# Attention, a SoLU layer and a top-1 expert layer on one core: w_out centred over its rows, the norm's factor applied after the second product, h as one tile over two PSUM banks

## The chip, the cores and the metric

One core of a Trainium2 chip runs the whole program. The metric is device time in microseconds (us), the median of three runs. Engines: TensorE (PE; its weight loads are listed as PEld), VectorE (DVE), ScalarE (ACT), GpSimd (POOL), and SyncE (SP), which only issues transfers. Each engine works through its own list of instructions in a fixed order.

## The reference, cut to what matters

```python
attn = softmax(mask(q @ k.T / 8)) @ v            # 4 batches, 8 heads, 768 positions, 64 wide
x = attn.reshape(3072, 512)
h = x @ w_in                                      # 512 -> 1024
e = np.exp(h - h.max(-1)); sm = e / (e.sum(-1) + 1e-9)
solu = h * sm
ln = (solu - solu.mean(-1)) / np.sqrt(solu.var(-1) + 1e-6) * g_ln
x = ln @ w_out                                    # 1024 -> 512
idx = argmax(x @ w_gate); gate = softmax(x @ w_gate)[idx]
out = gate * (relu(x @ w1[idx]) @ w2[idx])        # 8 experts
```

## The kernel before, in words

**Attention** works in 32 units (two heads, half a batch's positions). A unit is scores, row maximum (L226 on VectorE), exponential (L228 on ScalarE), transposes, product with v. Its result x is split into a high and a low part (bxh, bxl, L302 and L303).

**The SoLU layer** ("MoE 1") works in 24 tiles of 128 tokens. `m_in` multiplies x with w_in in two halves of 512 columns, three matmuls per slice for the high and low parts (L426 to L428); each half of the result is a PSUM bank of its own, `h`. `m_act` takes the row maximum of each half (L432), the exponential (L443), h times it (L445), the mean, the squares (L451, which write over h), then y = 1/sqrt(variance) with a Newton step, and in L460 the normalised e = e*y + mean*y. `m_tr` transposes e (L475) and splits it into lh and ll (L478, L479). `m_out` multiplies with w_out (L496 to L498), whose 264 columns hold 256 of w_out and 8 router logits in the first half; L504 to L512 are the router's small vector steps; `m_route` ranks the token within its expert (L521, L522). `m_in` runs two tiles ahead of `m_out`.

**Weights** arrive as 64-bit floats. `decode` (L316 to L333) fetches 512 KB, and rebuilds 32-bit values on VectorE, ScalarE and GpSimd. `load_w_in` and `load_w_out` split them into high and low parts (wih and wil, woh and wol). `load_w_out` also scales by g_ln (L370, L371), transposes w_out (L349) and multiplies it with w_gate (L357), so that the logits come out of the same matmul.

**The experts** ("MoE 2") follow: `f_in` (L779 to L781) and `f_out` (L828 to L830).

**Order.** The generators `attention()`, `moe1()` and `weights()` are stepped in turn. For the first 110 attention steps (C0) only attention and weights are stepped: w_in's eight steps first, one in six attention steps (WSTEP), then w_out's from step 62 (C1). After that attention and MoE 1 share by a ratio (RATIO). A scheduler that reckons with a timeline of its own then sets each engine's order. PSUM has 8 banks; `ps` hands out 3 to the tag "psa" (attention) and 5 to "psm" (MoE 1 and decoding), and rotates over both in the experts.

Of the kernel before, what the change touches and what calls it, by code (L numbers as in the profile page):

```python
# [29 lines left out]
NPT, XBUFS, QKB, PKB, VB = 2, 8, 2, 2, 2  # L30
WB, DB, EB, NXR, XGB = 3, 4, 2, 2, 6
PA = 3
NATP = 3
KLV = 2
LA = 2
# [5 lines left out]
C0, C1, WSTEP, WSTEP2, RATIO = 110, 62, 6, 2, 0.7  # L41
# [11 lines left out]
def body(ctx, tc, a):  # L53
# [6 lines left out]
    ps_p = ctx.enter_context(tc.tile_pool(name="ps", bufs=8, space=PSUM))  # L60
# [3 lines left out]
    def open_moe1(where, sfx):  # L64
# [4 lines left out]
        wil = w1p.tile([128, 4, DF], F32R, name="wil" + sfx)  # L69
# [239 lines left out]
    wg_sb = const.tile([128, 4, NE], F32, name="wg_sb")  # L309

# [5 lines left out]
    def decode(src, sb=None):  # L316
# [15 lines left out]
        V.scalar_tensor_tensor(out=y, in0=x, scalar=E_MIN, in1=t.bitcast(F32), op0=ALU.is_ge, op1=ALU.mult)  # L332
        return y  # L333

    def load_w_in():
        for k in range(4):
# [7 lines left out]
    def load_w_out():  # L344
        def logits(k, x):

            t = ps("wt")
            for d in range(4):
                T.transpose(t[:, 128 * d:128 * d + 128], x[:, 128 * d:128 * d + 128], ident)  # L349
            xt = dec_tile("xt").bitcast(F32).rearrange("p (a b) -> p a b", a=4)  # L350
            A.activation(out=xt, in_=t.rearrange("p (a b) -> p a b", a=4), func=AF.Copy)
            return k, xt

        def logits2(k, xt):
            t = ps("wt2")
            for d in range(4):
                T.matmul(t[:, 0:NE], xt[:, d, :], wg_sb[:, d, :], start=(d == 0), stop=(d == 3))  # L357
            wp = t[:, 0:NE]
            gk = g_sb[:, k:k + 1]
            V.tensor_scalar(out=woh[:, k, 0, 256:264], in0=wp, scalar1=gk, scalar2=None, op0=ALU.mult)  # L360
            V.scalar_tensor_tensor(out=wol[:, k, 0, 256:264], in0=wp, scalar=gk, in1=raw(woh)[:, k, 0, 256:264],
                                   op0=ALU.mult, op1=ALU.subtract)

        last = last2 = None
        for k in range(8):
            x = dec_tile("dec").bitcast(F32)
            decode(a["w_out"].bitcast(I32)[128 * k:128 * k + 128, :], x)
            h_ = woh[:, k, :, 0:256]
            p2 = x.rearrange("p (a b) -> p a b", a=2)
            A.activation(out=h_, in_=p2, func=AF.Copy, scale=g_sb[:, k:k + 1])  # L370
            V.scalar_tensor_tensor(out=wol[:, k, :, 0:256], in0=p2, scalar=g_sb[:, k:k + 1], in1=raw(h_),  # L371
                                   op0=ALU.mult, op1=ALU.subtract)
            if last2:
                logits2(*last2)
                last2 = None
            if last:
                last2 = logits(*last)
            last = (k, x)
# [40 lines left out]

    def m_in(t, c):  # L420
        xh, xl = xs_t[t]
        h = ps("h")
        h_t[t, c] = h
# [6 lines left out]
        if c == 0:  # L430
            sc_t[t] = mp.tile([128, 12], F32, tag="sc", name="sc", bufs=LA)
        V.tensor_reduce(out=sc_t[t][:, c:c + 1], in_=h, axis=AX.X, op=ALU.max, negate=True)  # L432
# [3 lines left out]
    def m_act(t):  # L436
        sc = sc_t.pop(t)
        nm, sm, mu, v_, y, w_, es = [sc[:, j:j + 1] for j in (0, 2, 4, 6, 8, 9, 10)]
# [841 lines left out]
```

## Time and profile before

| | us |
|---|---|
| median of 3 runs | 839.29 (838.95 to 845.25) |
| the profiled execution | 835.08 |
| its span | 833.4 |
| TensorE busy in it | 783.8 (94%) |
| VectorE, ScalarE, GpSimd busy | 469.0, 470.7, 380.0 |

The span is the time between the first and the last recorded instruction; the profiled execution's own time is 1.7 us longer. A matmul's end is modelled, so a busy TensorE isn't one at its peak. Granted clock 1.00 is TensorE's 2.4 GHz, 0.50 is 1.2 GHz. In a row of waits the engine before the arrow sat idle until the instruction behind it ended.

### The profile page before, as it was taken

How to read it: one execution, taken by the hardware profiler on the slowest of the kernel's cores; microseconds unless marked ns; L12 is line 12 of the kernel's file. 1: busy time of each engine (PE TensorE's matmuls, PEld its weight loads, DVE VectorE, ACT ScalarE, POOL GpSimd, SP SyncE). 2: the span in 40 equal slices, each digit the busy share in tenths (PEclk: the TensorE clock that was granted, in tenths of full speed). 3: DMA queues.
4: the chain of work that ended last, by engine and by line, in shares of the span. 5: the costliest groups of instructions: out<-in, count | busy, mean ns of one | idle time of the engine just before them, and what ended most of it. 6: DMA issues, size and time to landing. Idle time of an engine off the chain costs nothing.

```text
span 833.4 us, 15246 instructions
## 1 busy us (share of the span) xinstructions
PE 783.8 (94%) x4906; PEld 681.7 (82%) x4906; DVE 469.0 (56%) x1730; ACT 470.7 (56%) x1224; POOL 380.0 (46%) x419
## 2 busy tenths in 40 slices
PE   3479999899999999999999989999999999999996
PEld 2258888788898887888988879989988898989885
DVE  6779674776757747666776475425414332435421
ACT  4686685676766847757766364235314342435532
POOL 4777356454544554545443021157225253526433
PEclk9986999999999999999999999999999999999999
DMA  8687456677555557564431270286325353536320
GB/s 271 194 208 184 104 157 96 174 136 141 143 138 143 126 117 149 134 148 122 126 75 40 22 246 27 54 279 224 115 89 171 101 176 117 174 116 201 129 103 18
DMA packets 77385, 114.36 MB, mean 137 GB/s; under 512 B 14125, under 2 KB 53485, under 8 KB 77296
## 3 DMA queue, kind: packets, MB, share of 16 engines
q1 hardware_dynamic: 69456, 91.02, 42.6%
q0 software_dynamic: 5248, 13.88, 4.7%
q10 hardware_dynamic: 2592, 8.39, 3.0%
q8 instruction: 41, 0.67, 0.4%
q14 instruction: 48, 0.39, 0.3%
HBM read 72.22 MB, written 13.94 MB: 103 GB/s over the span
## 4 chain that ended last, share of the span: by engine, by line
PE 77%; DMA 10%; DVE 5%; issue 4%; ACT 2%; POOL 1%; POOLq 0%; SPq 0%; ACTq 0%; DVEq 0%
PE x L496 5%; PE ht L780 5%; PE ht L779 5%; PE ht L781 5%; PE x L498 5%; PE x L497 5%; PE y L830 5%; PE h L426 5%; PE y L829 5%; PE y L828 5%; PE av L297 5%; PE h L427 5%; PE h L428 4%; PE s L221 3%; DMA w<-w_in 2%
## 5 line engine op out<-in xcount | busy, mean ns | idle before, releaser
L496 PE MATMUL x<-woh,lh 128*128 128x264 f32 (+1 forms) x384 | 112.0, 292 | 0.5 <-DVE ll L479 0.4
L228 ACT ACTIVATE P<-P,mx 128x144 f32<-128x144 f32 x192 | 78.7, 412 | 55.5 <-DVE mx L226 52.9
L498 PE MATMUL x<-woh,ll 128*128 128x264 f32 (+1 forms) x384 | 110.0, 287 | 0.0
L497 PE MATMUL x<-wol,lh 128*128 128x264 f32 (+1 forms) x384 | 109.4, 285 | 0.0
L700 POOL TENSOR_TENSOR wl<-wst,wh 128x1024 fp32r<-128x1024 f32 x28 | 68.5, 2445 | 63.2 <-ACT wh L694 63.0
L694 ACT ACTIVATE wh<-wst 128x1024 fp32r<-128x1024 f32 x64 | 67.5, 1058 | 46.5 <-PE ht L780 33.9
L828 PE MATMUL y<-wh,hh 128*128 128x512 f32 x224 | 89.8, 401 | 0.0
L830 PE MATMUL y<-wh,hl 128*128 128x512 f32 x224 | 88.1, 395 | 0.1
L829 PE MATMUL y<-wl,hh 128*128 128x512 f32 x224 | 87.6, 392 | 0.0
L700 DVE TENSOR_TENSOR wl<-wst,wh 128x1024 fp32r<-128x1024 f32 x36 | 54.7, 1526 | 51.1 <-ACT wh L694 51.0
L780 PE MATMUL ht<-xel,wh 128*128 128x288 f32 (+5 forms) x256 | 81.2, 318 | 0.0
L781 PE MATMUL ht<-xeh,wl 128*128 128x288 f32 (+5 forms) x256 | 81.0, 318 | 0.0
L779 PE MATMUL ht<-xeh,wh 128*128 128x288 f32 (+5 forms) x256 | 79.7, 318 | 0.0
L426 PE MATMUL h<-wih,bxh 128*128 128x512 f32 x192 | 78.1, 407 | 0.8 <-DVE ll L479 0.8
L186 POOL TENSOR_TENSOR lA<-qd,qA 128x384 fp32r<-128x384 f32 x29 | 29.7, 1024 | 105.1 <-ACT qA L184 104.5
L225 DVE COPY_PREDICATED s<-pick,s 128x128 f32<-128x128 int32 x160 | 45.5, 292 | 54.2 <-PE s L222 51.7
L427 PE MATMUL h<-wil,bxh 128*128 128x512 f32 x192 | 76.0, 396 | 0.0
L496 PEld LDWEIGHTS x<-woh,lh 128*128 128x128 f32 x384 | 72.9, 190 | 1.8 <-DVE ll L479 0.5
L428 PE MATMUL h<-wih,bxl 128*128 128x512 f32 x192 | 73.9, 398 | 0.0
L497 PEld LDWEIGHTS x<-wol,lh 128*128 128x128 f32 x384 | 73.0, 190 | 0.8
L498 PEld LDWEIGHTS x<-woh,ll 128*128 128x128 f32 x384 | 72.8, 190 | 0.4 <-issue 0.2
L835 ACT ACTIVATE y<-y,gate 128x512 f32<-128x512 f32 x28 | 19.3, 688 | 92.9 <-PE y L830 69.4
(243 smaller groups left out, 2094.4 us busy)
## 6 DMA issues: line engine op xcount, KB each, us to landing
wst<-w SPq DMA_DIRECT2D x64, 512.0 KB
x_d<-xrow SPq DMA_DIRECT2D x24, 264.0 KB
qd<-qT SPq DMA_DIRECT2D x32, 192.0 KB
qB<-qA SPq DMA_DIRECT2D x58, 96.0 KB
lB<-lA SPq DMA_DIRECT2D x58, 96.0 KB
kd<-kx SPq DMA_DIRECT2D x16, 280.0 KB
w<-w_in ACTq DMA_DIRECT2D x8, 512.0 KB
w<-w_out ACTq DMA_DIRECT2D x8, 512.0 KB
```

The costliest lines, as they stand in the source:

```text
L426: T.matmul(h, xh[k], wih[:, k, cs], start=(k == 0), stop=False)
L427: T.matmul(h, xh[k], wil[:, k, cs], start=False, stop=False)
L496: T.matmul(p[:, 0:n], lh[:, k, :], woh[:, k, c, 0:n], start=(k == 0), stop=False)
L497: T.matmul(p[:, 0:n], lh[:, k, :], wol[:, k, c, 0:n], start=False, stop=False)
L498: mm = T.matmul(p[:, 0:n], ll[:, k, :], woh[:, k, c, 0:n], start=False, stop=(k == 7))
L700: return (G if c % 2 and r else V).tensor_tensor(out=l_, in0=st_w.pop((r, which, c)), in1=raw(h_), op=ALU.subtract)
L779: T.matmul(o, wh[:, k, fs], xh(k), start=(k == 0), stop=False)
L780: T.matmul(o, wh[:, k, fs], xl(k), start=False, stop=False)
L781: T.matmul(o, wl[:, k, fs], xh(k), start=False, stop=(k == 3))
L828: T.matmul(o, hh[:, k, sl], wh, start=(k == 0), stop=False)
L829: T.matmul(o, hh[:, k, sl], wl, start=False, stop=False)
L830: T.matmul(o, hl[:, k, sl], wh, start=False, stop=(k == 7))
```

## The change

- w_out is decoded first into an 8-slice tile (wox) that shares its memory with wil; the mean over its 1024 rows of g*w_out is made on TensorE (`mean`: g/1024 broadcast as weights), and each slice is centred (`xc`) before it is split. The logit columns are centred in the same way. w_in is decoded after that. Steps come one in four attention steps, 24 in all.
- With a centred w_out the mean of solu need not be subtracted: `m_act` leaves out L459 and L460, and the factor y is applied where ScalarE copies the second product out (scale=y) and in the router's shift.
- h is one tile of 1024 columns over two PSUM banks, in a buffer of its own (tag "psh", one buffer); the maximum, exponential, product and square are one instruction each instead of two.
- The router's small tensors L and M lie in spare columns of the product's PSUM bank.
- PSUM: "psa" 3 banks, "psm" 3, "psh" 2, where the experts use psh's two halves in turn.

```diff
-PA = 3
-C0, C1, WSTEP, WSTEP2, RATIO = 110, 62, 6, 2, 0.7
+C0, WSTEP, WSTEP2, RATIO = 110, 4, 2, 0.7
...
+        return ps_p.tile([128, 512], F32, tag=tag, name=name, bufs=3)
+    def ps2(name):
+        return ps_p.tile([128, 1024], F32, tag="psh", name=name, bufs=1)
...
     def load_w_out():
+        mn = ps2("mn")
+        x8 = w1p.tile([128, 8, 2, 256], F32, tag="wil", name="wox")
...
+        def mean(k, out, x):
+            T.matmul(out, g_m[:, k:k + 1].to_broadcast([128, 128]), x, start=(k == 0), stop=(k == 7),
+                     skip_group_check=True)
...
+        for k in range(8):
             h_ = woh[:, k, :, 0:256]
-            A.activation(out=h_, in_=p2, func=AF.Copy, scale=g_sb[:, k:k + 1])
-            V.scalar_tensor_tensor(out=wol[:, k, :, 0:256], in0=p2, scalar=g_sb[:, k:k + 1], in1=raw(h_),
-                                   op0=ALU.mult, op1=ALU.subtract)
+            xc = ps("xc")
+            V.scalar_tensor_tensor(out=xc.rearrange("p (a b) -> p a b", a=2), in0=xs[k], scalar=g_n[:, k:k + 1],
+                                   in1=mn[:, 0:512].rearrange("p (a b) -> p a b", a=2), op0=ALU.mult, op1=ALU.add)
+            xc = xc.rearrange("p (a b) -> p a b", a=2)
+            A.activation(out=h_, in_=xc, func=AF.Copy)
+            V.tensor_tensor(out=wol[:, k, :, 0:256], in0=xc, in1=raw(h_), op=ALU.subtract)
...
     def m_in(t, c):
-        h = ps("h")
-        h_t[t, c] = h
+        if c == 0:
+            h_t[t] = ps2("h")
+        h = h_t[t][:, 512 * c:512 * c + 512]
...
-        V.tensor_reduce(out=sc_t[t][:, c:c + 1], in_=h, axis=AX.X, op=ALU.max, negate=True)
...
     def m_act(t):
+        ef = e.rearrange("p a b -> p (a b)")
+        V.tensor_reduce(out=nm, in_=h, axis=AX.X, op=ALU.max, negate=True)
+        A.activation(out=ef, in_=h, func=AF.Exp, bias=nm, accum_out=sm)
+        acted.append(V.scalar_tensor_tensor(out=ef, in0=h, scalar=ES, in1=ef, op0=ALU.mult, op1=ALU.mult,
+                                            accum_out=mu))
+        st_t[t] = e
+        A.activation(out=h, in_=ef, func=AF.Square, bias=mu, scale=-1.0 * DF, accum_out=v_)
...
-        V.tensor_scalar(out=mu, in0=mu, scalar1=32.0, scalar2=y, op0=ALU.mult, op1=ALU.mult)
-        acted.append(A.activation(out=e, in_=e, func=AF.Identity, scale=y, bias=mu))
-        st_t[t] = e
...
-            A.activation(out=xr[:, 256 * c:256 * c + 256], in_=p[:, 0:256], func=AF.Copy)
+            A.activation(out=xr[:, 256 * c:256 * c + 256], in_=p[:, 0:256], func=AF.Copy, scale=y)
...
-                lg = p[:, 256:264]
+                lg, L = p[:, 256:264], p[:, 264:272]
...
     def weights():
+        yield from load_w_out()
         yield from load_w_in()
-        yield from load_w_out()
```

**VectorE, the weights of MoE 1.** The kernel before, around w_out's first slices; dt, dec and dh are steps of the decoding, wil and wol the low parts, P and mx attention's rows.

```order
L225 COPY_PREDICATED s<-pick,s 128x128
L341 TENSOR_TENSOR wil<-dh,wih 128x512
L332 SCALAR_TENSOR_TENSOR dec<-dh,dec 128x512
L326 SCALAR_TENSOR_TENSOR dec<-w_851,dt 128x512
L226 ISA P,mx<-s,mk 128x144
L226 ISA mx 128x1
L324 TENSOR_SCALAR dt<-w_915 128x512
L371 SCALAR_TENSOR_TENSOR wol<-dec,g_sb,woh 128x2x256
```

This wil is w_in's last; each slice of w_out is split as soon as it is decoded, and the first maximum of h stands at row 225 of VectorE.

The same engine now, where w_out's slices are centred (xc) and split (wol), all eight having been decoded; wlg are the logit columns:

```order
L240 RECIPROCAL sm<-sm 128x6
L308 TENSOR_TENSOR bxl<-av,bxh 128x384
L401 SCALAR_TENSOR_TENSOR xc<-wox,g_n,mn 128x512 x2
L407 TENSOR_TENSOR wlg<-wlg,g_n 128x64
L230 COPY_PREDICATED s<-pick,s 128x128 x3
L405 TENSOR_TENSOR wol<-xc,woh 128x2x256
L408 TENSOR_TENSOR wlg<-wlg,mn 128x64
L401 SCALAR_TENSOR_TENSOR xc<-wox,g_n,mn 128x512
```

w_in's decoding begins 29 rows behind this piece, its last wil stands 81 rows further, and the first maximum of h at row 248. Ahead of that maximum stand 47 pairs of L231 (L226 before) instead of 38, 39 copies instead of 31, and 5 bxl instead of 4.

**TensorE, tile 0 and tile 1 of MoE 1.** Before, where tile 0's second half and tile 1's first meet (h is a product with w_in, s are scores):

```order
L426 MATMUL h<-wih,bxh 128x512
L427 MATMUL h<-wil,bxh 128x512
L221 MATMUL s<-kA,qA 128x272
L222 MATMUL s<-kA,lA 128x272
L428 MATMUL h<-wih,bxl 128x512 x2
```

Halves of two tiles are filled in turn, each in a bank of its own.

Now, the last rows ahead of tile 1's first matmul (L460); lt are the transposes of tile 0's e:

```order
L499 MATMUL lt<-ident,e 128x128 x8
L226 MATMUL s<-kA,qA 128x272
L227 MATMUL s<-kA,lA 128x272
L226 MATMUL s<-kB,qB 128x272
L227 MATMUL s<-kB,lB 128x272
L460 MATMUL h<-wih,bxh 128x512
L461 MATMUL h<-wil,bxh 128x512
```

Between tile 0's last matmul and this L460 stand these, and six more score matmuls, six transposes of attention and one unit's product with v: tile 1 waits for tile 0's h to be free.

**TensorE, the last but one tile of m_in.** Before, ahead of tile 22's first matmul (x is the product with w_out, ct counts the experts' tokens):

```order
L498 MATMUL x_6555<-woh,ll 128x256
L606 LDWEIGHTS ones_b
L606 MATMUL ct<-acc,ones_b 128x8
L426 MATMUL h<-wih,bxh 128x512
L427 MATMUL h<-wil,bxh 128x512
```

The last rows are tile 22's first matmuls, into banks that tile 21 doesn't hold.

The same place now:

```order
L522 MATMUL x_6305<-woh,ll 128x256
L631 LDWEIGHTS ones_b
L631 MATMUL ct<-acc,ones_b 128x8
L499 MATMUL lt<-ident,e 128x128 x8
L460 MATMUL h<-wih,bxh 128x512
L461 MATMUL h<-wil,bxh 128x512
```

Here lt are tile 20's transposes, which stood behind the first half of tile 22 before; between tile 21's last matmul and L460 stand 30 matmuls of m_out, the small rk and ct, and these eight, with no attention left.

## Rows read from the trace of the kernel before

**Rows 1.** The page: busy time; TensorE and its clock in 40 slices.

```profile
PE 783.8 (94%) x4906; PEld 681.7 (82%) x4906; DVE 469.0 (56%) x1730; ACT 470.7 (56%) x1224; POOL 380.0 (46%) x419
...
PE   3479999899999999999999989999999999999996
...
PEclk9986999999999999999999999999999999999999
```

**Rows 2.** Windows: busy us (instructions) by engine, granted clock, DMA share, GB/s.

```profile
0.00:50.00 50.00, 22.51 (x73) 12.60 (x73) 38.10 (x121) 30.79 (x78) 31.44 (x77) 1.00 0.72 226
...
60.00:80.00 20.00, 18.13 (x90) 16.26 (x91) 17.96 (x49) 13.55 (x34) 13.61 (x13) 0.57 0.76 187
...
90.00:530.00 440.00, 430.71 (x3024) 378.93 (x3023) 290.91 (x1290) 291.60 (x890) 191.88 (x227) 1.00 0.52 121
530.00:804.00 274.00, 273.18 (x1493) 242.33 (x1492) 103.37 (x216) 110.84 (x168) 118.47 (x83) 1.00 0.47 153
804.00:833.40 29.40, 21.93 (x122) 18.25 (x120) 4.85 (x4) 8.48 (x11) 9.60 (x6) 0.94 0.08 31
```

**Rows 3.** Waits of PE from 90 to 530 us: total, times, longest; ten rows.

```profile
PE rk L521 <- DVE ll L479: 2.3, 1, 2.3
...
PE s L222 <- DMA lA<-lA: 0.6, 1, 0.6
...
PE tp L275 <- DVE mx L226: 0.3, 1, 0.3
```

**Rows 4.** Windows within the start.

```profile
59.00:61.00 2.00, 0.26 (x2) 0.06 (x1) 1.48 (x2) 1.61 (x5) 1.93 (x3) 1.00 0.73 168
...
62.00:78.00 16.00, 15.07 (x70) 13.75 (x71) 15.03 (x43) 12.04 (x30) 10.48 (x10) 0.50 0.74 186
```

**Rows 5.** Groups of VectorE, 0 to 90 us: count, busy us, mean ns, idle before.

```profile
L226 DVE CUSTOM_DVE_ANT_0 P<-s,mk 128x144 f32<-128x144 f32 x36 | 10.1, 296 | 0.1
L371 DVE SCALAR_TENSOR_TENSOR wol<-dec,g_sb,woh 128x512 fp32r<-128x512 f32 x8 | 8.2, 1029 | 4.3 <-ACT woh L370 4.3
L225 DVE COPY_PREDICATED s<-pick,s 128x128 f32<-128x128 int32 x28 | 7.8, 287 | 1.6 <-PE s L222 1.5
...
L341 DVE TENSOR_TENSOR wil<-dh,wih 128x512 fp32r<-128x512 f32 x8 | 5.5, 683 | 0.2 <-ACT wih L340 0.2
...
L226 DVE DVE_READ_ACCUMULATOR2_ANT mx<- 128x1 f32 x36 | 2.9, 81 | 0.0
...
L360 DVE TENSOR_SCALAR woh<-wt,g_sb 128x8 fp32r<-128x8 f32 x8 | 1.8, 220 | 0.6 <-PE wt L357 0.6
```

**Rows 6.** Groups of the whole span, same columns.

```profile
L297 PE MATMUL av<-pt,vd 128*64 128x256 f32 (+1 forms) x448 | 47.1, 351 | 0.0
...
L275 PE MATMUL tp<-ident,pk 128*128 128x128 f32 x192 | 32.4, 290 | 8.3 <-DVE skt L263 5.7 <-POOL pk L237 1.2 <-DVE sc L459 0.6
...
L460 ACT ACTIVATE e<-e,sc 128x1024 f32<-128x1024 f32 x24 | 29.4, 1237 | 5.9 <-DVE sc L459 5.9
...
L218 PE MATMUL s<-kd,qd 64*128 64x272 f32 x36 | 14.4, 722 | 17.0 <-DVE mx L226 7.8 <-DMA kd<-kx 6.2 <-ACT pt L276 1.8
...
L357 PE MATMUL wt<-wg_sb,xt 128*128 128x8 f32 x64 | 11.1, 302 | 1.6 <-ACT xt L351 1.6
```

**Rows 7.** Timeline of one tile: start us, us, engine, line.

```profile
224.16 0.39 PE L428 MATMUL h<-wih,bxl 128*128 128x512 f32 x1
224.38 0.28 PE L496 MATMUL x<-woh,lh 128*128 128x264 f32 x1
224.50 0.29 PE L497 MATMUL x<-wol,lh 128*128 128x264 f32 x1
...
224.58 0.69 DVE L432 TENSOR_REDUCE sc<-h 128x1 f32<-128x512 f32 x1 [0.91 <-PE h L428]
...
225.50 0.69 ACT L443 ACTIVATE e<-h,sc 128x512 f32<-128x512 f32 x1 [2.55 <-DVE sc L441]
...
229.76 0.67 ACT L451 ACTIVATE h<-e,sc 128x512 f32<-128x512 f32 x1
```

More of the change, by code (lines that the diff above doesn't have):

```diff
@@ L331, in decode @@
         y = x if sb is None else sb
-        V.scalar_tensor_tensor(out=y, in0=x, scalar=E_MIN, in1=t.bitcast(F32), op0=ALU.is_ge, op1=ALU.mult)
+        t = t.bitcast(F32)
+        if sb is not None:
+            x, t = [v_.rearrange("p (a b) -> p a b", a=2) for v_ in (x, t)]
+        V.scalar_tensor_tensor(out=y, in0=x, scalar=E_MIN, in1=t, op0=ALU.is_ge, op1=ALU.mult)
         return y
     def load_w_in():
+        nonlocal wil
+        wil = w1p.tile([128, 4, DF], F32R, tag="wil", name="wil")
         for k in range(4):
@@ L364, in load_w_out @@
[L364 to L378 removed]
+                T.matmul(mn[:, 512 + 8 * k:520 + 8 * k], xt[:, d, :], wg_sb[:, d, :], start=(d == 0), stop=(d == 3))
@@ new lines, in mean @@
+        def mean(k, out, x):
+            T.matmul(out, g_m[:, k:k + 1].to_broadcast([128, 128]), x, start=(k == 0), stop=(k == 7),
+                     skip_group_check=True)
+        last = None
+        for k in range(8):
+            decode(a["w_out"].bitcast(I32)[128 * k:128 * k + 128, :], xs[k])
+            if last:
+                logits2(*last)
+                last = None
+            if k:
+                mean(k - 1, mn[:, 0:512], xs[k - 1])
+                last = logits(k - 1)
+            yield 1.5
@@ new lines, in load_w_out @@
+        logits2(*last)
+        mean(7, mn[:, 0:512], xs[7])
+        logits2(*logits(7))
+        wl = dec_p[0].tile([128, 8, NE], F32, tag="wlg", name="wlg")
+        A.activation(out=wl, in_=mn[:, 512:576].rearrange("p (k e) -> p k e", k=8), func=AF.Copy)
+        for k in range(8):
+            mean(k, mn[:, 576:576 + NE], wl[:, k])
+        for k in range(8):
+            h_ = woh[:, k, :, 0:256]
+            xc = ps("xc")
[4 more added lines that the diff above has]
+            V.tensor_tensor(out=wol[:, k, :, 0:256], in0=xc, in1=raw(h_), op=ALU.subtract)
+            if k == 1:
+                V.tensor_tensor(out=wl, in0=wl, in1=g_n.unsqueeze(2).to_broadcast([128, 8, NE]), op=ALU.mult)
+                V.tensor_tensor(out=wl, in0=wl, in1=mn[:, 576:576 + NE].unsqueeze(1).to_broadcast([128, 8, NE]),
+                                op=ALU.add)
+                V.tensor_copy(woh[:, :, 0, 256:264], wl)
+                V.tensor_tensor(out=wol[:, :, 0, 256:264], in0=wl, in1=raw(woh)[:, :, 0, 256:264], op=ALU.subtract)
@@ L429, in m_in @@
             yield 0.65
[L430 to L432 removed]
     acted = []
     def m_act(t):
[L437 to L439 removed]
+        sc = mp.tile([128, 8], F32, tag="sc", name="sc", bufs=LA + 2)
+        nm, sm, mu, b_, y, w_, v_ = [sc[:, j:j + 1] for j in range(7)]
@@ L1189, in body @@
             late_loads()
-        if cnt_ % WSTEP == 0 and (wn[0] < 8 or C1 <= cnt_ and wn[0] < 16):
+        if cnt_ % WSTEP == 0 and wn[0] < 24:
             step(gw, "w")
             wn[0] += 1
-    for _ in range(max(0, 16 - wn[0])):
+    for _ in range(max(0, 24 - wn[0])):
         step(gw, "w")
@@ L1226, in body @@
     open_h()
+    halves[0] = True
     moe2()
+    halves[0] = False
     c_ctx.close()
```

86 lines of the change are left out of this document (38 added, 48 removed).

## The prediction

> **What bounds the kernel now.** I read the page first: TensorE is busy 783.8 us of 833.4, no other engine over 57% [rows 1]. So only what TensorE does, waits for, or does at half clock can move the end. Then the windows by stage [rows 2]. From 530 to 804 us (the experts) TensorE is busy 273.2 of 274.0: nothing to win there. From 90 to 530 us (MoE 1 with attention) it is busy 430.7 of 440.0, and VectorE and ScalarE, each at about 291 of 440, have a third of their time free. The start is different: in the first 50 us TensorE works 22.5 us and VectorE 38.1; from 60 to 80 VectorE is busy 18.0 of 20. The end, 804 to 833, isn't touched by the change.
>
> The waits of TensorE in the middle come next [rows 3]: ten rows from 2.3 us down to 0.3, together 9.1 us, of which all but the 0.6 for the lA transfer end with VectorE or with ScalarE's L460. This is the most that a lighter MoE 1 can win there. Last, two windows inside the start [rows 4]: after a stretch in which TensorE worked 0.26 of 2 us, it runs at a granted clock of 0.50, that is 1.2 GHz, from 62 to 78 us, and is busy 15.07 of those 16: work of 7.5 us at full clock, so 7.5 us are lost to the clock there if TensorE was the bound, which its busy share suggests.
>
> **The start, part by part.** Before, w_in is decoded first, and the first product h waits for attention's first units and then flows from about 90 us. Now w_in comes last, its low part even uses the memory that w_out's decoded slices leave, so the first complete h waits for the whole chain: decode w_out, mean, centre, decode w_in. VectorE is what this stage runs on, so I count its list up to the first maximum of h, by the order: nine more pairs of score instructions, 9 x (0.296 + 0.081) = 3.4 us; eight more copies, 8 x 0.287 = 2.3 us; sixteen instructions of 512 elements (xc and wol, priced like L341, 0.683) = 10.9 us in place of eight L371 (1.029) = 8.2 us, so +2.7; one bxl more, taken at 0.6; the sixteen small instructions like L360 (0.220) go and five come, -2.4 [rows 5]. Sum +6.6 us. VectorE was busy 56.1 of 70 us in the stretches 0 to 50 and 60 to 80 [rows 2], 80%; at that pace it is +8.2 us until h flows.
>
> Against it stands work that TensorE has then already done. The nine pairs and the bxl belong to attention: one product with v (47.1/32 = 1.5 us, and its first two matmuls, about 0.6), one unit's transposes (32.4/32 = 1.0) [rows 6], and eighteen score matmuls of 272 columns at some 0.12 us each, the spacing of a 264-column matmul [rows 7], 2.2 us. Together 5.3 us; I take 5, and it is not done later again.
>
> The mean adds eight matmuls of fp32 with 512 columns, and eight of 8 columns. No row shows the former. From below: two passes of a 512-column matmul at the spacing of 0.22 us [rows 7], 8 x 0.44 = 3.5 us. From above: L218, also fp32, 14.4 us for 18 matmuls of 272 columns [rows 6], so 8 x 0.8 x 512/272 = 12 us. I take the upper, its row is the same kind of matmul. The small ones, priced like L357 with its two records for each, are 8 x 2 x 0.302 at most, 5 us, less if they overlap [rows 6]. All of it stands within the first fifty-odd rows of TensorE, beside the 27.5 us that TensorE idles in the first 50 us [rows 2], so I cost it at nothing; were the cover gone it would cost up to 17 us.
>
> The clock: the transposes and small matmuls of w_out (L349, L357), which filled TensorE between 60 and 80 us at half clock, now stand much earlier, where the clock was 1.00 and TensorE had idle time [rows 2]. What is left at 60 to 80 us is attention's alone, for which VectorE is later anyway. I give back 5.5 of the 7.5 us lost; the bounds are all of it, and nothing.
>
> Start: +8.2 - 5 - 5.5 = -2.3 us. The bounds: with VectorE fully used +6.6 - 5 - 7.5 = -6; with nothing back from the clock +3; with the mean uncovered besides, +20.
>
> The rule that speaks against this step: the Trainium skill (TensorE: Matmul & The Clock Gate, HAM oscillation) says that gaps in the matmul stream put the array back to half rate, each time anew. The trace agrees in that the half clock from 62 us follows two nearly idle us [rows 4]. By that rule a start in which TensorE waits for VectorE's centring could stay at half clock for longer, and the sum would be without the -5.5. That case is the third rival.
>
> **MoE 1's tiles.** From each of 24 tiles go: L460 (1.237 us of ScalarE, 29.4 in all [rows 6]), four small instructions of VectorE, and the second halves' fixed costs. None of it lies on TensorE's path, which is busy 98% there; it is worth what it takes off the 9.1 us of waits [rows 3]. VectorE's bursts of maxima and products from two tiles at once, which stand behind these waits, get shorter by about a third, and L460 no longer stands ahead of the transposes. I take two thirds of the 8.5 us, -5.7; bounds 0 and -8.5.
>
> The price is that h has one buffer. The next tile's first matmul waits until the square that overwrites h (L451 before, L478 now) is done. Before, the chain from a tile's last product to its last square took from 224.55 to 230.43, 5.9 us, in a quiet tile [rows 7]. Now the maximum covers both halves after the last matmul (about +0.6, L432 is 0.69 per half), the product waits for the whole exponential (+0.6), and three small steps of the mean go (-0.5): 6.6 us. What TensorE has to do meanwhile stands in its list. In the middle of the stage 41 to 48 matmuls of m_out at 0.12 us [rows 7], and some 2.5 us of attention: 7 to 9.7 us, 8.4 typically, so the wait is hidden. Not so at three places. Between tiles 0 and 1: ten score matmuls (1.2), fourteen transposes (at 0.1, 1.4) and one product with v (2.1) make 4.7, so 1.9 us are missing. Between tiles 21 and 22: 30 matmuls of m_out (3.6), two small ones and eight transposes, 4.7 again, 1.9 missing. Between 22 and 23, 48 matmuls and little else, 6.5: 0.1 missing. I add 1 us for the other tiles. Cost +4.9. Behind the next tile's first matmul, when it waits, TensorE's whole list stands still, attention too.
>
> The factor y rides on the copy that is there already; its chain is two tiles old by then. The router's shift from PSUM costs VectorE about what it cost before; it keeps one bank longer, and "psm" has three. The experts' order is the same apart from names, and no stage there waits for a bank now. I cost these at nothing; m_out's 5 us beside them are the cover, and a wait per tile of 0.3 would cost 7.
>
> MoE 1: -5.7 + 4.9 = -0.8 us.
>
> **Sum.** -2.3 - 0.8 = -3.1 us. The profiled execution took 835.08 us, its span 833.4 and 1.7 around it; with the change 832.0. The median of the runs is 839.29, 4.2 above the profiled one, and what is measured is a median: 839.29 - 3.1 = 836.2.
>
> **Rivals.**
> First, faster: the start gains its -6 and the middle all of its 8.5, the chain of h being hidden but for 3 us: -11.5, so 827.8. For it: VectorE's spare third [rows 2]. Against it: h now comes last in the weights.
>
> Second, slower: h's single buffer. Between two tiles everything depends on one chain of four long instructions on two queues, each with attention's instructions ahead of it. In the quiet tile the chain was 6 us, but VectorE and ScalarE are two thirds busy [rows 2], and each of the four steps can find 0.4 to 0.7 us of other work in front: 6.6 + 4 x 0.6 = 9.0 us. Against 8.4 us of cover that is 0.6 us in each of 20 gaps, 12.0, and at the three short places 2.4 more each, 3.9 + 7.2 = 11.1. The middle then gives -5.7 + 23.1 = +17.4, with the start's -2.3 it is +15.1: 854.4. It decides from a chain of 8.4 us on. For it: the in-order queues; against it: TensorE standing still lets both engines catch up.
>
> Third, no change: the clock stays at half in the start, so -3.1 + 5.5 = +2.4: 841.7.
>
> **How the numbers follow.** A measurement of this kernel can tell about 1% from no change, 8.4 us. Forecast 0.38, the first rival 0.32, the second 0.20, the third 0.10. The forecast and the third lie within 1%; the forecast's own spread (827 to 845) puts a little of it below the lower bound, and the second rival gives a little back above: faster 0.34, same 0.45, slower 0.21. For the range I leave out a tenth on each side: half of the second rival's upper part, and what lies beyond the first: 823 to 852. The forecast's own range is 827 to 845.
>
> **What would show it.** The start: the first maximum of h at most 8 us later than before, a granted clock over 0.8 from 60 to 80 us, and TensorE's mean matmuls done by about 45 us. The middle: waits of TensorE for VectorE under 4 us, for the square L478 some 5, at the three short places. I am wrong in the start if that maximum comes 14 us later or more, or if half clock fills 60 to 90 us; in the middle if TensorE waits for L478 in most tiles, or if other waits of over 3 us come up, such as for a bank of "psm".

## The result, and the profile after

Over 20 runs of each the changed kernel took 850.62 us, the kernel before 842.0: a ratio of 1.006 [1.0031 to 1.0089]. In a second set (ten runs and seventeen) it was 844.64 against 836.39, 1.0081 [1.0043 to 1.0119]. The ratios leave out runs over 1.5% above the fastest of their kernel, which are six of the changed kernel's first twenty and none of the other's; the medians with all of them lie 8.6 and 8.3 us apart. So by the ratios the change costs 5 to 7 us: within the 1% that the forecast took for no change, inside its range, and with the wrong sign.

The profiled execution of the changed kernel took 849.17 us, its span 847.5; a second one, of the second set, 848.19 and 846.5. Against the span before the difference is 14.1 and 13.1 us, more than the ratio says, since the profiled execution before lies 7 us under the median of its 20 runs. What follows is read as where time goes, and its sum is too large by that much.

The page after:

```profile
PE 796.3 (94%) x4938; PEld 687.9 (81%) x4938; DVE 451.7 (53%) x1536; ACT 437.4 (52%) x1105; POOL 378.6 (45%) x419
...
PE   5877699999999998999999989989999999999996
...
PEclk9896799999999999999999999989999999999999
```

VectorE and ScalarE have less to do (469.0 and 470.7 in [rows 1]). TensorE's busy time went up by 12.5 us. Its clock is low in the fourth and fifth slices (64 to 106 us); before, it was low in the fourth alone.

The windows after, with the columns of [rows 2]:

```profile
0.00:50.00 50.00, 37.73 (x175) 23.84 (x176) 29.63 (x112) 29.38 (x77) 30.89 (x78) 0.93 0.70 219
60.00:80.00 20.00, 13.26 (x51) 9.38 (x52) 20.00 (x63) 15.57 (x43) 11.63 (x12) 0.59 0.68 181
80.00:100.00 20.00, 12.66 (x65) 8.49 (x66) 16.68 (x47) 14.54 (x37) 14.01 (x15) 0.73 0.80 207
...
90.00:530.00 440.00, 425.63 (x2958) 374.20 (x2959) 273.15 (x1066) 258.32 (x767) 190.44 (x220) 0.98 0.54 119
530.00:804.00 274.00, 270.69 (x1466) 240.10 (x1466) 101.78 (x236) 108.35 (x168) 117.68 (x87) 0.99 0.46 147
```

In the first 50 us VectorE is busy 29.63 us (38.10 before), from 60 to 80 all of the 20. TensorE's clock in 60 to 80 is 0.59, as before (0.57); from 80 to 100 it is busy 12.66 us at 0.73. The same window before, and the middle:

```profile
80.00:100.00 20.00, 19.83 (x120) 16.64 (x120) 13.21 (x55) 11.14 (x36) 8.88 (x12) 1.00 0.46 121
120.00:480.00 360.00, 354.13 (x2514) 309.23 (x2513) 237.33 (x1064) 241.40 (x747) 165.98 (x195) 1.00 0.54 120
```

The same windows of the second profile of the changed kernel:

```profile
0.00:50.00 50.00, 38.20 (x120) 22.68 (x121) 27.90 (x102) 25.26 (x66) 26.75 (x73) 0.78 0.64 202
60.00:80.00 20.00, 13.46 (x78) 9.88 (x77) 17.25 (x50) 14.03 (x41) 10.20 (x11) 0.66 0.60 149
80.00:100.00 20.00, 10.87 (x46) 6.90 (x45) 17.08 (x55) 12.36 (x32) 15.75 (x16) 0.73 0.81 215
120.00:480.00 360.00, 358.06 (x2546) 314.91 (x2545) 228.25 (x914) 216.82 (x664) 167.38 (x198) 1.00 0.55 119
```

TensorE's waits from 90 to 530 us, after (columns of [rows 3]):

```profile
PE s L227 <- DMA lA<-lA: 5.4, 4, 2.5
PE h L460 <- ACT wih L356: 4.6, 1, 4.6
PE x L520 <- DVE ll L503: 3.9, 1, 3.9
```

The first maximum of h, VectorE's timeline, first before and then after:

```profile
94.25 0.69 DVE L432 TENSOR_REDUCE sc<-h 128x1 f32<-128x512 f32 x1
```

```profile
104.15 1.22 DVE L473 TENSOR_REDUCE sc<-h 128x1 f32<-128x1024 f32 x1
```

It is 9.9 us later (19.4 in the second profile, at 113.61). Two profiles of one kernel lie 9.5 us apart here, and each run below has one profile: a smaller difference in this maximum is not enough to name a cause.

Since busy time contains half clock, I counted work: each matmul of attention, MoE 1 and the experts, by its start, at the spacing that its kind has at full clock (0.23 us for 512 columns, 0.12 for x). Every kernel has 723 to 724 us of it. Done by that time, in us:

| kernel | by 120 us | by 480 | by 800 |
|---|---|---|---|
| before | 46.4 | 388.3 | 698.5 |
| after, first profile | 40.5 | 381.7 | 685.3 |
| after, second profile | 31.1 | 379.9 | 684.8 |

So the start loses 5.9 and 15.3 us, the middle (120 to 480) loses 0.7 in the first profile and gains 6.9 in the second, and 480 to 800 loses 6.6 and 5.3. The sums, 13.2 and 13.7, are nearly the differences of the spans, 14.1 and 13.1.

### The profile page after: what moved, and what is told of

Its sections match the earlier page's. It is cut to its first block, busy times and chain, and to the rows that moved or that the text cites. A ratio compares the mean times of both kernels' runs of the same rounds, so it can differ in the third digit from the quotient of the medians.

```text
span 847.5 us, 14986 instructions
## 1 busy us (share of the span) xinstructions
PE 796.3 (94%) x4938; PEld 687.9 (81%) x4938; DVE 451.7 (53%) x1536; ACT 437.4 (52%) x1105; POOL 378.6 (45%) x419
## 4 chain that ended last, share of the span: by engine, by line
PE 70%; DMA 12%; issue 4%; ACT 1%; DVE 1%; SPq 1%; POOL 0%; POOLq 0%; ACTq 0%
PE x L520 5%; PE ht L804 5%; PE ht L806 5%; PE ht L805 5%; PE x L522 5%; PE x L521 4%; PE y L853 4%; PE y L854 4%; PE y L855 4%; PE h L460 4%; PE h L462 4%; PE h L461 4%; PE av L302 4%; DMA lA<-lA 3%; DMA lB<-lA 3%
## 5 line engine op out<-in xcount | busy, mean ns | idle before, releaser
L725 POOL TENSOR_TENSOR wl<-wst,wh 128x1024 fp32r<-128x1024 f32 x28 | 68.1, 2431 | 63.8 <-ACT wh L719 63.6
L719 ACT ACTIVATE wh<-wst 128x1024 fp32r<-128x1024 f32 x64 | 67.7, 1059 | 50.6 <-PE ht L805 37.6
L460 PE MATMUL h<-wih,bxh 128*128 128x512 f32 x192 | 79.4, 413 | 6.0 <-ACT wih L356 6.0
L853 PE MATMUL y<-wh,hh 128*128 128x512 f32 x208 | 83.7, 404 | 0.0
L855 PE MATMUL y<-wh,hl 128*128 128x512 f32 x208 | 82.6, 398 | 0.1
L854 PE MATMUL y<-wl,hh 128*128 128x512 f32 x208 | 82.2, 396 | 0.0
L725 DVE TENSOR_TENSOR wl<-wst,wh 128x1024 fp32r<-128x1024 f32 x36 | 53.4, 1490 | 51.7 <-ACT wh L719 51.6
L461 PE MATMUL h<-wil,bxh 128*128 128x512 f32 x192 | 77.8, 405 | 0.8 <-DVE wil L357 0.8
L462 PE MATMUL h<-wih,bxl 128*128 128x512 f32 x192 | 77.5, 403 | 0.0
L806 PE MATMUL ht<-xeh,wl 128*128 128x288 f32 (+5 forms) x240 | 76.1, 318 | 0.0
L805 PE MATMUL ht<-xel,wh 128*128 128x288 f32 (+5 forms) x240 | 76.0, 318 | 0.0
L804 PE MATMUL ht<-xeh,wh 128*128 128x288 f32 (+5 forms) x240 | 74.6, 319 | 0.0
L861 POOL DMA_INDIRECT out<-y,dst x28 | 31.1, 1112 | 83.2 <-ACT y L860 73.2
```

The source lines that it names most:

```text
L460: T.matmul(h, xh[k], wih[:, k, cs], start=(k == 0), stop=False)
L461: T.matmul(h, xh[k], wil[:, k, cs], start=False, stop=False)
L725: return (G if c % 2 and r else V).tensor_tensor(out=l_, in0=st_w.pop((r, which, c)), in1=raw(h_), op=ALU.subtract)
L804: T.matmul(o, wh[:, k, fs], xh(k), start=(k == 0), stop=False)
L805: T.matmul(o, wh[:, k, fs], xl(k), start=False, stop=False)
L806: T.matmul(o, wl[:, k, fs], xh(k), start=False, stop=(k == 3))
```

## The experiments

Two questions were open: which part of the start is slow, and why the middle gives its gain in one profile and not in the other. Ratios are to the kernel before, run beside it. e5, e6, e8, e13 and e14 leave solu's mean in x; the others, but for e1, compute the whole. e3, e7, e9, e10, e11, e15 and e18 came out slower than every range set for them.

### One part alone

```diff
 e2: before's tiles (m_in, m_act, m_out, PSUM pools), after's load_w_out and order
-WS = 2.0 ** 14
+WS = -1.0
...
+        mn, ml = ps("mn"), ps("mn")
```

> The new start alone: w_out first, mean and centring, w_in after it; the tiles of MoE 1, h in halves and the PSUM tags as in the kernel before (the mean stands in two banks of psm). Start theory: first maximum of h 8 to 12 us later than before, half clock again between 60 and 100 us, ratio 1.003 to 1.010. Tile theory: the work done ahead by attention pays for the later h, no waits over 2 us behind 110 us, ratio 0.996 to 1.002.

1.0076 [1.0046 to 1.0106], first maximum at 100.50, 6.3 us later. The start by itself costs what the whole change costs.

```diff
 e1: after's tiles; before's load order, decoding and late loads
...
-        yield from load_w_out()
         yield from load_w_in()
+        yield from load_w_out()
```

> The change without its new start: w_in is decoded first and into its own memory, w_out as in the kernel before, neither centred nor preceded by mean matmuls (the mean of solu is thus left in); the tiles of MoE 1 as in the change. Start theory (the loss comes from w_out first, mean and centring): first maximum of h at about 94 us as before, no waits of TensorE over 2 us behind 110 us, ratio to the kernel before 0.985 to 1.000. Tile theory (the loss comes from h's one buffer and the tiles' new timing, as in the waits of 2.2, 2.5, 3.9 and 2.8 us behind 300 us): such waits again, ratio 1.003 to 1.012.

1.3034, 1102.58 us: a miss. The logits also kept solu's mean, so tokens went to other experts, and a fallback for full experts ran after some 850 us. It tells nothing of the tiles. In its place, with the logit columns corrected by the mean (cb holds minus their column means):

```diff
 e5: e1, and in m_out
-                lg, L = p[:, 256:264], p[:, 264:272]
+                lg, L = p[:, 280:288], p[:, 264:272]
+                V.scalar_tensor_tensor(out=lg, in0=cb, scalar=mu, in1=p[:, 256:264], op0=ALU.mult,
+                                       op1=ALU.add)
...
```

> The start of the kernel before (w_in first, no mean, no centring of w_out) with the tiles of the change, h as one tile in one buffer; only the eight logit columns are centred (by 8 matmuls of 8 columns and one small step of VectorE per tile), so the mean of solu stays in the rest of x. If start and tiles add up (start alone +0.76%, change +0.6%): 0.998 to 1.000, first maximum of h at 94 to 96 us. If h's one buffer and the PSUM left for the rest cost more with the old start: 1.004 or more.

1.0086 [1.0042 to 1.013]; waits for the lA transfer 5.5 us, first maximum 98.16.

```diff
 e6: e5 with h in halves, five banks of "psm"
...
-            h_t[t] = ps2("h")
+        h = ps("h")
+        h_t[t, c] = h
```

> The same with h in halves and five banks for psm, as in the kernel before; the mean is not subtracted from solu, except in the logits. If the parts add up: 1.000 - 0.0076 = 0.992, range 0.989 to 0.996. If the gain of the fourth run came from the new start and not from the tiles: 0.998 or more.

1.0126 [1.0086 to 1.0167]; no waits for lA, but 5.7 us for the router's rank product and 3.4 for skt.

```diff
 e4: after, h in halves, five banks of "psm" (PSUM pools as before), the logits in a tile apart from mn
-        mn = ps2("mn")
+        mn, ml = ps("mn"), ps("mn")
...
-            h_t[t] = ps2("h")
+        h = ps("h")
+        h_t[t, c] = h
```

> The change with h in two banks of psm (five banks) taken by halves as before, so the next tile doesn't wait for the square; the mean is still not subtracted. Theory that h's one buffer costs the time: ratio 0.990 to 1.000. Start theory: first maximum still about 10 us later than before, ratio 1.003 to 1.010, waits for L478 were 0.3 us in the change and can give nothing back.

1.0000 [0.9972 to 1.0028], the only whole version that costs nothing. Waits for lA 0.3 us; instead, TensorE's waits for the bank of a rank product:

```profile
PE x L523 <- DVE r L555: 7.5, 6, 1.7
```

So the parts don't add: the start alone is +0.8%, the tiles alone +0.9% (one h) or +1.3% (halves), both together 0.0% (halves) or +0.6% (one h). "The tiles alone" have one small VectorE step per tile more than the change, the correction of the logits; what it costs was not tried.

### The start

```diff
 e3: w_in decoded first; wox lies in the tiles lh, ll, e
-        x8 = w1p.tile([128, 8, 2, 256], F32, tag="wil", name="wox")
+        x8 = [mp.tile([128, 2, 2, 256], F32, tag=t_, name="wox") for t_ in ("lh", "ll", "e", "e")]
...
+        yield from load_w_in()
         yield from load_w_out()
-        yield from load_w_in()
```

> The change with w_in decoded first; w_out is still centred, but its decoded slices lie in memory that lh, ll and e use later, so wil has its own. Start theory with the order as its cause: first maximum of h back at about 95 us, ratio 0.990 to 1.001. Start theory with the centring as its cause (VectorE's list as long in any order): maximum still later than 100 us, ratio 1.003 to 1.008. Tile theory: ratio 1.003 to 1.009 whatever the start does.

1.0209 [1.016 to 1.0258], first maximum 102.34. The order of the two matrices isn't it: with w_in first, wil is done by 44 us, and yet TensorE begins h at 94.2, behind the xc (83 to 93 us), which now stand in dense work.

```diff
 e8: after without the mean and without xc (x keeps solu's mean)
-                mean(k - 1, mn[:, 0:512], xs[k - 1])
-        mean(7, mn[:, 0:512], xs[7])
...
-            xc = ps("xc")
+            A.activation(out=h_, in_=xs[k], func=AF.Copy, scale=g_n[:, k:k + 1])
+            V.scalar_tensor_tensor(out=wol[:, k, :, 0:256], in0=xs[k], scalar=g_n[:, k:k + 1], in1=raw(h_),
+                                   op0=ALU.mult, op1=ALU.subtract)
```

> The change without the eight mean matmuls of 512 columns and without centring the 512 columns of w_out (each slice is scaled and split by ScalarE and VectorE as in the kernel before); order of the weights, logits and tiles as in the change. The mean of solu is thus left in x. If the order (w_in last) makes the start late: ratio 1.003 to 1.007, first maximum at 98 us or later. If centring and mean make it late: 0.997 to 1.001, first maximum by 97 us.

1.0035 [1.0001 to 1.0069], first maximum 87.34, earlier than before the change: the maximum as the second expectation had it, the ratio as the first, so an early first product alone did not make the kernel faster. To be told apart were then the mean's TensorE work and xc itself:

```diff
 e13: e8 with the mean computed and not used
+                mean(k - 1, mn[:, 0:512], xs[k - 1])
+        mean(7, mn[:, 0:512], xs[7])
```

> The run of the order alone with the eight mean matmuls of 512 columns put back, their result unused (nothing waits for it; w_out's 512 columns are not centred, the mean of solu stays in x). If TensorE's time for the mean is what makes the start of the change late: first maximum of h at 98 us or later (87.3 without, 104 and 114 in the change), ratio 1.006 or more. If not: by 92 us, ratio 1.000 to 1.006.

```diff
 e14: after with a mean of zero
+        V.memset(mn[:, 0:512], 0.0)
-                mean(k - 1, mn[:, 0:512], xs[k - 1])
-        mean(7, mn[:, 0:512], xs[7])
```

> The change without the eight mean matmuls of 512 columns; each slice still passes through xc in PSUM, with zeros in the mean's place, so VectorE's list is as long as in the change but nothing waits for all eight slices' mean (the 512 columns are not centred, the mean of solu stays in x). If VectorE's eight longer steps and xc's banks make the start late: first maximum at 98 us or later, ratio 1.005 or more. If the wait for the mean does: by 92 us, ratio 1.000 to 1.005.

e13: 0.9968 [0.9935 to 1.0000], first maximum 97.48. e14: 1.0146 [1.0102 to 1.019], 108.11. With the mean's wide matmuls and no xc the loss is gone; with xc and no wide mean it is there, 1.8% apart on one chip. So the way through xc is what costs, not TensorE's time for the mean (e13's maximum lies 10 us behind e8's all the same). Tiles of the start, first after (count: ns least/median/most, first and last start):

```profile
L346 DVE SCALAR_TENSOR_TENSOR wox<-dh,dec x8: 648/684/692, 14.4 to 44.9; 128x512 f32<-128x512 f32 x8
L378 PE MATMUL mn<-wox,g_m x16: 592/676/1220, 15.6 to 50.0; 128*128 128x512 f32 x16
L401 DVE SCALAR_TENSOR_TENSOR xc<-wox,g_n,mn x8: 739/741/757, 56.3 to 68.6; 128x512 f32<-128x512 f32 x8
L405 DVE TENSOR_TENSOR wol<-xc,woh x8: 673/676/678, 58.8 to 70.7; 128x512 fp32r<-128x512 f32 x8
L357 DVE TENSOR_TENSOR wil<-dh,wih x8: 674/684/692, 77.4 to 101.9; 128x512 fp32r<-128x512 f32 x8
```

e8:

```profile
L399 DVE SCALAR_TENSOR_TENSOR wol<-wox,g_n,woh x8: 744/906/1477, 17.4 to 47.6; 128x512 fp32r<-128x512 f32 x8
L357 DVE TENSOR_TENSOR wil<-dh,wih x8: 677/682/692, 55.6 to 81.5; 128x512 fp32r<-128x512 f32 x8
```

e13:

```profile
L378 PE MATMUL mn<-wox,g_m x16: 592/1061/1220, 15.7 to 56.7; 128*128 128x512 f32 x16
L401 DVE SCALAR_TENSOR_TENSOR wol<-wox,g_n,woh x8: 740/1076/2064, 17.0 to 55.3; 128x512 fp32r<-128x512 f32 x8
L357 DVE TENSOR_TENSOR wil<-dh,wih x8: 643/691/692, 62.0 to 89.7; 128x512 fp32r<-128x512 f32 x8
```

e14:

```profile
L400 DVE SCALAR_TENSOR_TENSOR xc<-wox,g_n,mn x8: 743/748/756, 57.7 to 70.1; 128x512 f32<-128x512 f32 x8
L357 DVE TENSOR_TENSOR wil<-dh,wih x8: 680/682/692, 79.7 to 101.0; 128x512 fp32r<-128x512 f32 x8
```

Where a slice can be split as it is decoded (e8, e13), wol runs beside the decoding and wil is done by 82 to 90. Where xc stands between, all eight wait until 56 or 58, and wil, whose memory wox holds until the last xc has read it, begins at 77 to 80. Whether that memory holds wil or only the order of the decodings was not tried apart.

With a mean of zero the xc come no earlier, but e14 still waits for a mean, that of the logit columns. Its 16 small matmuls write the second bank of mn, the tile whose first bank xc reads. First after, then e14, then e4, which keeps the logits in a tile of their own (ml); of each the matmuls of TensorE and the first xc of VectorE:

```profile
54.35 1.95 PE L378 MATMUL mn<-wlg,g_m 128*128 128x8 f32 x16
56.34 1.42 DVE L401 SCALAR_TENSOR_TENSOR xc<-wox,g_n,mn 128x512 f32<-128x512 f32 x2 [0.23 <-PE mn L378]
```

```profile
54.25 3.42 PE L379 MATMUL mn<-wlg,g_m 128*128 128x8 f32 x16
57.70 1.42 DVE L400 SCALAR_TENSOR_TENSOR xc<-wox,g_n,mn 128x512 f32<-128x512 f32 x2 [1.54 <-PE mn L379]
```

```profile
44.81 1.12 PE L373 MATMUL mn<-wox,g_m 128*128 128x512 f32 x2
45.97 0.76 DVE L396 SCALAR_TENSOR_TENSOR xc<-wox,g_n,mn 128x512 f32<-128x512 f32 x1
56.14 1.85 PE L373 MATMUL mn<-wlg,g_m 128*128 128x8 f32 x16
```

In e4 the first xc starts as soon as the mean over w_out is done, 10 us ahead of the logits' means; in the change that mean is done at 50.6 us and the xc start at 56.3. Where mn is one tile (after, its second profile, e3, e11, e14, e15) it starts within 0.3 us of the last of the small matmuls. So the first xc waits for the logits through a shared tile. e14 therefore doesn't part this wait from xc's own eight instructions and their banks, and no run has the change with two tiles and nothing else, so what the wait costs in the end is not shown.

```diff
 e15: the weights' steps closer together
-C0, WSTEP, WSTEP2, RATIO = 110, 4, 2, 0.7
+C0, WSTEP, WSTEP2, RATIO = 110, 3, 2, 0.7
```

> The change with the weights' steps one in three attention steps instead of one in four (WSTEP 3), which puts three attention units' score pairs fewer ahead of the first maximum. If the start's lateness is VectorE's list ahead of that maximum: 1 to 3 us earlier, ratio 1.002 to 1.006. If it is the chain decode, mean, centring, decode, whatever the list: first maximum at 103 us or later, ratio 1.005 to 1.010.

1.0255 [1.0219 to 1.029], first maximum 113.11: less attention in VectorE's list ahead of h, and it comes no earlier than in the change (104 and 114). Nothing here says that a shorter list helps.

```diff
 e18: e4's work; eight decodings of w_out, all of w_in, then the centring, whose eight steps
      come behind the attention-only stretch; wox has memory of its own
...
+        go = load_w_out()
+        for _ in range(8):
+            yield next(go)
         yield from load_w_in()
+        yield from go
...
-        if cnt_ % WSTEP == 0 and wn[0] < 24:
+        if cnt_ % WSTEP == 0 and wn[0] < 16:
```

> The fourth run (change with h in halves, ratio 1.000, first maximum 98.6 us) with all its work, but w_in is decoded between w_out's decoding and its centring, so that the first product doesn't wait for the centring; w_out's decoded slices lie in memory of lh, ll, e and one tile of their own. If the serial order decode w_out, centre, decode w_in is what makes the start late: first maximum at 86 to 93 us with mean and xc as long as in the change, ratio 0.988 to 0.998. If the amount of VectorE's work does: first maximum at 96 us or later, ratio 0.999 to 1.006.

```profile
L397 DVE SCALAR_TENSOR_TENSOR xc<-wox,g_n,mn x8: 743/745/756, 83.7 to 105.8; 128x512 f32<-128x512 f32 x8
L352 DVE TENSOR_TENSOR wil<-dh,wih x8: 643/684/692, 56.4 to 82.9; 128x512 fp32r<-128x512 f32 x8
```

1.0087 [1.0054 to 1.0119]; first maximum 95.42, between the two expectations (e4: 98.62). wil no longer waits for the centring, and the time is met again behind it, in xc and in the middle (348.75 us busy from 120 to 480). That the centring ahead of w_in makes wil late is shown, and taking it away isn't enough to win; the first maximum, 3 us earlier than e4's, is within what two profiles of one kernel differ by.

### Centring e instead of w_out

```diff
 e7: e6 without cb; e centred on VectorE
+        acted.append(V.tensor_scalar(out=ef, in0=ef, scalar1=1.0 * DF, scalar2=mu, op0=ALU.mult, op1=ALU.subtract))
 e16: e8 with the same line, and the logit columns not centred
-            mean(k, mn[:, 576:576 + NE], wl[:, k])
 e9: e7 with w_out decoded first, and the rank product's bank, rk, moved to "psa"
-        yield from load_w_in()
         yield from load_w_out()
+        yield from load_w_in()
-    ATT, MOE, flip = ("s", "tp", "skp", "av"), ("h", "lt", "x2", "wt", "wt2", "rk", "dt", "dh"), [0]
+    ATT, MOE, flip = ("s", "tp", "skp", "av", "rk"), ("h", "lt", "x2", "wt", "wt2", "dt", "dh"), [0]
 e17: e9 with the ATT line as in e7
```

> A version with the whole computation that could beat both: the start of the kernel before, h in halves, y applied at the exit, and the mean taken off e by one VectorE instruction of 1024 elements per tile behind the square, in place of L460 on ScalarE. Theory that L460's place on ScalarE ahead of the transposes was the cost, and that VectorE has room in the middle: 0.992 to 0.996. Theory that any pass over e in the chain costs as much: 0.998 to 1.002.

> A version with the whole computation that could beat both: order of the weights and tiles of the change, no mean matmuls and no centring of w_out; VectorE takes the mean off e (1024 elements, some 1.1 us per tile) behind the square. If the early start of the order alone (first maximum 87 us) is kept and VectorE's room in the middle hides 24 x 1.1 us: 0.995 to 1.003. If the longer chain from the square to the transposes is met by TensorE at the end of MoE 1 and between tiles: 1.005 to 1.012.

> A version with the whole computation: w_out first, but scaled and split slice by slice with no mean and no centring, so no step waits for all eight slices; w_in after it; the mean taken off e by one VectorE instruction per tile; h in halves; the router's rank product in a bank of psa, so that the second half of x doesn't wait for its reader. Theory that the barrier of mean and centring made the start late: first maximum of h by 92 us, more work done at 120 us than in the kernel before. If the tiles then keep clear of the waits of the fourth run: 0.988 to 0.997. If some other wait takes their place: 1.000 to 1.010.

> A version with the whole computation: w_out first, scaled and split slice by slice without mean or centring; h in halves with five banks of psm, the rank product in psm; the mean taken off e by one VectorE instruction per tile (the ninth run with its rank product back in psm). If its early start is kept and the rank product in psa was the ninth run's cost: first maximum of h by 98 us, 0.992 to 1.003. If halves with this start meet the waits of the ninth run anyway: 1.015 or more.

1.0122 [1.0078 to 1.0165], 1.0034 [1.0003 to 1.0065], 1.0363 [1.0307 to 1.0419] and 1.0085 [1.0051 to 1.0118]; first maxima 102.64, 89.98, 96.70 and 99.19. e16 computes everything without xc, with an early h like e8's, and still isn't faster than before. The surprise is e9 against e17: one small product's bank, 2.8%. The same edit on e4:

```diff
 e10: e4 with
-    ATT, MOE, flip = ("s", "tp", "skp", "av"), ("h", "lt", "x2", "wt", "xc", "mn", "rk", "dt", "dh"), [0]
+    ATT, MOE, flip = ("s", "tp", "skp", "av", "rk"), ("h", "lt", "x2", "wt", "xc", "mn", "dt", "dh"), [0]
```

> The fourth run (change with h in halves) with the router's rank product in psa in place of psm. If the waits of x for the step r behind it (7.5 us there, six times) go and nothing takes their place: 0.990 to 0.995. If attention's scores wait for that bank in their place: 0.998 to 1.003.

1.0353 [1.0305 to 1.04]. It was to take away the 7.5 us of e4, and cost 3.5%. e10's window:

```profile
120.00:480.00 360.00, 341.22 (x2380) 294.21 (x2379) 229.68 (x991) 217.66 (x708) 164.09 (x196) 0.98 0.52 119
```

### The waits for lA

lA is attention's low part, copied by a transfer behind the loads of v, q and k on SP's queue.

```diff
 e11: after, these loads issued only behind the last copy
+        with behind():
+            SY.dma_start(out=qd, in_=qT[b, 2 * j:2 * j + 2, :, 384 * hf:384 * hf + 384].rearrange("r d s -> (r d) s"))
...
```

> The change with the loads of q, k and v for the next unit issued behind the copies of lA on SyncE's queue. If the waits of TensorE for lA (5.4 us, with half clock behind the two long ones) come from these loads being in flight ahead of the copies: waits for lA under 1.5 us, ratio 0.996 to 1.002. If the copies are late for another reason, or the loads are then late in their place: lA or qd and kd waits of 4 us and more, ratio 1.004 to 1.012.

1.0611 [1.0563 to 1.0659]. The waits for lA go, and these come:

```profile
PE s L233 <- ACT pt L288: 14.0, 3, 6.2
PE x L527 <- ACT lh L509: 9.9, 4, 4.2
```

```diff
 e12: the changed kernel again, no edit
```

> The change itself again, for a second profile. If its waits belong to its order: waits for lA of 4 to 8 us, for ll at the end of MoE 1 of 2 to 5 us and for xg of 2 to 4 us again, first maximum of h at 102 to 106 us. If they are chance: other waits in other places, the first maximum alone the same.

The ratio repeats (1.0081), the waits don't: none for lA, and 358.06 us busy from 120 to 480 at full clock, in the second profile's window above. In the first:

```profile
120.00:480.00 360.00, 353.43 (x2496) 309.76 (x2495) 223.61 (x906) 212.71 (x648) 163.94 (x193) 0.99 0.55 117
320.00:325.00 5.00, 3.79 (x30) 2.84 (x29) 3.12 (x10) 2.84 (x9) 3.18 (x5) 1.00 0.65 176
325.00:330.00 5.00, 4.04 (x12) 3.31 (x13) 1.22 (x6) 1.01 (x4) 0.00 (x0) 0.66 0.63 141
```

One such wait: TensorE stands still for 1.2 of the 5 us to 325 and 1.0 of the next, 2.2 in all, and runs at 0.66 in the second, which is another (1 - 0.66) x 5 = 1.7 us. The Trainium skill (TensorE: Matmul & The Clock Gate, HAM oscillation) says that waits in the matmul stream put the array back to half rate, each time anew. The trace agrees in kind, though this gap of 2.2 us is shorter than the waits in the page's example.

The kernels with one h show such waits (after 5.4 us, e3 7.7, e5 5.5, e8 9.0, e16 6.2, e15 4.7), though not in every profile (e13 1.6, e14 3.0, the second of after none); with halves they are 0.3 at most (0.6 before), but for e9, e10 and e18 (3.3, 3.0 and 2.7). What makes the transfer late is not settled.

## Why the prediction was wrong, point by point

**The step that failed is the start's "+8.2 - 5 - 5.5 = -2.3 us"; counted as work done by 120 us it measured +5.9 and +15.3 in the two profiles.** The terms:

- "At that pace it is +8.2 us until h flows": 9.9 and 19.4. The new instructions cost what I took for them (xc 0.741 and wol 0.676 in the tile rows, against 0.683), but the list was reckoned as a bag of work at a constant 80%. It is a chain: all decoded by 45 us, xc from 56, wil from 77. In the first 50 us VectorE works 8.5 us less than before, and from 60 to 80 it has no free time in which to catch up (2.75 us in the second profile). e15, with a shorter list, was no earlier.
- "I take 5" for attention done ahead: by 80 us TensorE has done 14.4 us of work against 11.3, so 3.1 (about 0.5 in the second profile); by 100 it is 22.4 against 28.3, because it waits for wih and h in between.
- "I give back 5.5 of the 7.5 us lost" to the clock: nothing came back. That was the third rival's mechanism, and it went further: the clock is 0.73 from 80 to 100 too, where it was 1.00. While the xc begin, TensorE is busy 0.24 of 3 us, and behind that its clock is 0.53 (columns of [rows 2]):

```profile
57.00:60.00 3.00, 0.24 (x2) 0.02 (x1) 3.00 (x9) 1.20 (x2) 2.11 (x4) 1.00 0.80 191
60.00:62.00 2.00, 1.33 (x6) 1.36 (x7) 2.00 (x9) 1.66 (x7) 0.00 (x0) 0.53 0.80 200
```

  In e8, without xc, the clock is 0.83 from 60 to 80 and 0.91 from 80 to 100. In the first profile 9.9 - 3.1 - 0 = +6.8 is near the 5.9 counted, so the clock's 5.5 is the largest part of the miss there; in the second it is the first term.
- The mean's matmuls at nothing: right for the eight wide ones as TensorE's time. They are done by 51 us, not 45 (59 in the second profile), and e13 with them all is at 0.997. One leaves two records, together 1.10 us at a granted clock of 1.00 (at 49.5 us) and 2.05 at 0.50 (at 29.0 us); all eight take 10.7 us, near the 12 taken from above. Not right for the small ones of the logit columns: they take 2 us, but end only at 56.3, and the first xc waits for them. The step left that wait out.

My own tests say the same: the first maximum is past the 8 us that I allowed in both profiles, past the 14 only in the second, and 60 to 80 us is at 0.59 and 0.66 where I asked for over 0.8.

**MoE 1, "-5.7 + 4.9 = -0.8 us".** The second term was wrong in the good direction: TensorE waits 0.3 us in all for the square that frees h, at none of the three short places noticeably. So the second rival, 854.4 us by that chain, fell, and the 4.9 with it. (The cover of 7 to 9.7 us that the chain was set against is 7.4 to 8.3 by its own terms; with no wait to speak of, that changed nothing.) The first term has the right size where nothing else comes up: +6.9 us of work from 120 to 480 us in the second profile. TensorE idles 1.9 of these 360 us there and 5.9 before, so 4.0 are idle time that went; the rest I have not traced. In the first it is taken back by a wait that I had not seen, 5.4 us for lA with half clock behind it (the 0.6 of [rows 3]); "other waits of over 3 us" was the sign that I had set for being wrong there.

**"I cost these at nothing", for what follows MoE 1.** TensorE loses 5 to 7 us of work from 480 to 800. VectorE's and then TensorE's timeline, after:

```profile
498.36 3.50 DVE L725 TENSOR_TENSOR wl<-wst,wh 128x1024 fp32r<-128x1024 f32 x3
501.77 0.68 DVE L503 TENSOR_TENSOR ll<-lt,lh 128x512 fp32r<-128x512 f32 x1
...
497.57 1.04 PE L499 MATMUL lt<-ident,e 128*128 128x128 f32 x8
502.51 0.39 PE L520 MATMUL x<-woh,lh 128*128 128x264 f32 x1 [3.90 <-DVE ll L503]
```

Three splits of the experts' weights (L725) stand ahead of a tile's last ll, and TensorE waits 3.9 us (the 2.3 for ll in [rows 3] is the place before). The gather of the first expert tokens follows with 2.8, which was 0.7:

```profile
PE xt L767 <- DMA xg<-x_d,idx_i: 2.8, 1, 2.8
```

Those two are 6.7 us against 3.0; the rest fits the lower clock (0.99 against 1.00 from 530 to 804). Neither was tried alone, so about half of what the first profile loses has no experiment behind it.

**The forecast.** The third rival (841.7, +2.4 us) was nearest to the +5 to +7 that the ratios give. The largest single chance, 0.45, was on no change beyond 1%, which held by the ratios. That is partly luck: the start lost more than the third rival allowed, and the wait on h that was to cost 4.9 us didn't come.

## What to carry to other kernels

A step that needs all the pieces before it treats one is a barrier: follow its chain with the memory and the banks that its pieces share with the next step, instead of adding its instructions to a list that was busy 80%. Look at what else is written to the tile that the step reads: here xc waited for small matmuls into the other bank of mn. Moving w_out's small matmuls out of the stretch at half clock gave nothing back (0.57 before, 0.59 after); don't book it as a gain before the order shows what TensorE does in their place. Where TensorE is 94% busy and the other engines are ordered around it, parts don't add, and a lighter part can be paid for by a wait elsewhere: versions that compute the same thing went from 0.0% (e4) to +6.1% (e11) by their arrangement.

## What the runs showed of the hardware and was not expected

- Moving the bank of one small product into attention's three costs 2.8% (e17 to e9) and 3.5% (e4 to e10). TensorE is busy 341.22 of 360 us in the middle of e10. No single wait carries it.
- A wait of 2.2 us in dense work cost 1.7 us more in clock behind it.
- The same kernel, profiled twice, lost 5.9 or 15.3 us in its start and 0.7 or -6.9 in its middle, with spans 1 us apart.
- The start with two free banks more for "psm" (five; e2 and e4) reached the first maximum at 98 to 100 us, with three at 104 to 114. These two also keep the logits in a tile apart from mn, and their xc begin at 46 and 54 us instead of 56 and 64. No run parts the two, and that the banks are the cause is not shown.
